# Row sums of a softmax: their guard taken from a constant array instead of an immediate number

## The chip, the cores and the metric

The kernel runs on one core of a Trainium2 chip. The metric is device time in microseconds (us) from one execution of the whole program, given as the median of several runs; lower is better. The engines are TensorE (PE, with its weight loads as PEld), VectorE (DVE), ScalarE (ACT), GpSimd (POOL) and SyncE (SP), which here only issues DMA transfers.

## The reference

Attention with a window of 32 positions to either side and 32 global tokens, for 8 batches of 8 heads with 512 local tokens and a head size of 64, followed by a feed-forward network on all 4352 rows. Every softmax divides by its row sum plus a guard of 1e-9:

```python
def sm(s):
    s = s - np.max(s, axis=-1, keepdims=True)
    e = np.exp(s)
    return e / (np.sum(e, axis=-1, keepdims=True) + 1e-09)

out_g = sm(scale * q_g @ k_all.T) @ v_all
out_l = sm(concat([scale * q_l @ k_g.T, where(mask, scale * q_l @ k_l.T, -1e9)])) @ v_all
x = concat([out_g, out_l])            # heads joined: rows of 512
h = x @ w_in                          # 512 -> 2048
out = (h - np.tanh(h)) @ w_out        # 2048 -> 512
```

## The kernel before

All arithmetic is in float32. TensorE multiplies each float32 operand as a rounded part and a remainder (`x_hi`, `x_lo`, `w_in_hi`, `w_in_lo`, `w_out_hi`, `w_out_lo`, and `gates` in both parts), three products to one. The weights are split once, in the first sixth of the program.

Attention goes by head pairs. The first four pairs (eight heads) go one way: `add_local_scores` multiplies queries with keys for tiles of 128 rows and 224 columns; `add_scores` has DVE take the row maxima with the mask (`peak`, line 1104), ACT take the exponent with the row sums as a by-product (`exp`, line 1111), and then `add_norms` lets DVE add the guard to the row sums and invert them (`inverse`, lines 671 and 672), for a pair of heads and two tiles at once: 128 partitions by 2 by 2 numbers. POOL multiplies the rows with the inverses (`norm`, line 1117), and TensorE transposes them (line 1176). The other 28 pairs go another way: `add_band_scores` and `add_band` do the same for one head and its four row tiles of 128 columns (`peak` line 1132, `exp` line 1137, `inverse` lines 1141 and 1142 on 128 by 4 numbers, `norm` line 1146, and a transpose on DVE, line 1152). The rows of the global tokens have their own path (`Quad`, lines 982 to 1050), whose guard is added together with a second sum, by an instruction with two arrays and an immediate (lines 997 and 1046).

The feed-forward network of a batch runs beside the attention of the next one: line 1219 (or 1245 at the start) multiplies by the first weights, ACT takes the tanh (line 1227), DVE subtracts (line 1230), ACT and POOL split the result in two parts (lines 363 and 1236), line 1282 multiplies by the second weights. When the last head is done, only the network is left, from about 780 us on.

The order of the work on every engine is worked out while the program is built: every operation is put in by `add` with the engines that can do it and its estimated time, due time, the keys that it reads (`r`) and writes (`w`), and the planner (`Order.run`) places them one after the other. An operation with `lock=True`, and each one on POOL, is planned so as not to run beside another such one. `inverse` is one with `lock=True`. Where TensorE would have to wait long in the first 72 us, the planner puts in multiplications of an identity (line 1509) as filling.

All tiles stand in one pool, one after the other in each partition, in the order of the code: `stats` (the maxima, sums and inverses) is the first, `idr`, `rawkq` and the others follow. In the built program `stats` starts at byte 640 of the partition, `idr` at 896, `rawkq` at 1408.

Of the kernel before, what the change touches and what calls it, by code (L numbers as in the profile page):

```python
# [8 lines left out]
F32 = mybir.dt.float32  # L9
# [4 lines left out]
ALU = mybir.AluOpType  # L14
PSUM = bass.MemoryType.PSUM

P = 128
D = 64
# [5 lines left out]
def f32(ap):  # L24
    return ap.bitcast(F32)


def view(ap, dims, off=0):

    return bass.AP(ap.tensor, ap.offset + off, [list(ap.ap[0])] + [list(d) for d in dims])  # L30
# [19 lines left out]
class Order:  # L50
# [19 lines left out]
    def add(self, eng, fn, due, r=(), w=(), res=(), alloc=(), free=(), lat=0.0, xfer=0.0, rows=1.0, ldw=0.107, tail=0.226, lock=False, mode=0):  # L70
        o = Op()
        engs = [x + (0.0,) * (3 - len(x)) + (lock,) * (len(x) < 4) for x in (eng if isinstance(eng, list) else [eng])]
        o.eng = {x[0]: x[1:3] for x in engs}

        o.lock = {x[0] for x in engs if x[3] or x[0] == "P"}
        o.xfer, o.rows, o.ldw, o.tail, o.mode, o.land = xfer, rows, ldw, tail, mode, self.land
        o.fn, o.due, o.lat, o.alloc, o.free = fn, due, lat, alloc, free
        o.n, o.ready, o.succ, o.start, o.args, o.seq = 0, dict.fromkeys(o.eng, 0.0), {}, None, {}, len(self.ops)
        before = {}
        for k in tuple(r) + tuple(w) + tuple(res):  # L80
            if k in self.writer:
                before[id(self.writer[k])] = self.writer[k]
        for k in tuple(w) + tuple(res):
            for x in self.readers.get(k, ()):
                before[id(x)] = x
        for x in before.values():
            x.succ[id(o)] = o
            o.n += 1
        for k in r:
            self.readers.setdefault(k, []).append(o)  # L90
        for k in w:
            self.writer[k] = o
            self.readers[k] = []
        self.ops.append(o)
        return o
# [122 lines left out]
def kernel(ctx, tc, q_l, k_l, v_l, q_g, k_g, v_g, w_in, w_out, out):  # L218
    nc = tc.nc
    B, H, S, _ = q_l.shape  # L220
    G = q_g.shape[2]
    NT = S // P
# [6 lines left out]
    cp = ctx.enter_context(tc.tile_pool(name="cp", bufs=1))  # L229
# [7 lines left out]
    SQ = 4 * G  # L237
    stats_all = cp.tile([P, 4, 16], F32, name="stats")
    stats = [stats_all[:, j] for j in range(4)]
    idr = cp.tile([P, P], F32R, name="idr")  # L240
    idn = f32(idr)

# [114 lines left out]
    add = order.add  # L357
# [107 lines left out]
    def outside(x):  # L465
        return view(x[:, 0, 0:1], [(NT * KC - 2 * 32, 2), (1, 32)])
# [33 lines left out]
    class Pair:  # L500
# [163 lines left out]
        def add_norms(self, p):  # L664
            both = stats_all[:, self.heads[0].sn:self.heads[0].sn + 2]
            for a in self.heads:
                a.add_scores(p)

            def inverse(e, _):
                x, y = [both[:, :, a + 2 * p:a + 2 * p + 2] for a in (4, 8)]  # L670
                nc.vector.tensor_scalar(x, x, 1e-9, None, op0=ALU.add)
                nc.vector.reciprocal(y, x)

            n = [a.norms for a in self.heads]
            add(("D", 0.37), inverse, n[0][1] - 0.5, r=[x[3] for x in n], w=[x[2] for x in n], lock=True)
            for norm, due, st, x in n:
                add(("P", 0.89), norm, due, r=[st], w=[x])

# [385 lines left out]
    class Head:  # L1064
# [61 lines left out]
        def add_band(self, pair):  # L1126
            s, p, st = (f"s{self.two}", self.i), f"p{self.two}0", ("st0", self.sn)
            x = probs[self.two].rearrange("p (t c) -> p t c", t=NT)

            def peak(e, _):  # L1130
                for t in range(NT):
                    nc.vector.tensor_tensor_reduce(out=x[:, t], in0=self.scores[:, t], in1=bands[0 if t == 0 else 2 if t == NT - 1 else 1],  # L1132
                                                   scale=-0.125, scalar=1e30, op0=ALU.add, op1=ALU.min, accum_out=self.st[:, t:t + 1])

            def exp(e, _):
                for t in range(NT):
                    nc.scalar.activation(x[:, t], x[:, t], AF.Exp, bias=self.st[:, t:t + 1], scale=-1.0, accum_out=self.st[:, 4 + t:5 + t])  # L1137

            def inverse(e, _):
                y = self.st[:, 4:8]  # L1140
                nc.vector.tensor_scalar(y, y, 1e-9, None, op0=ALU.add)
                nc.vector.reciprocal(self.st[:, 8:12], y)  # L1142

            def norm(e, _):
                for t in range(NT):
                    nc.gpsimd.tensor_scalar(x[:, t], x[:, t], self.st[:, 8 + t:9 + t], 1.0, op0=ALU.mult, op1=ALU.mult)  # L1146

            def turn(e, _):
                y = pair.squares()
                n = 4 // len(y)  # L1150
                for k, z in enumerate(y):
                    nc.vector.transpose(z[:, :, self.two].rearrange("p n t c -> p t n c"),  # L1152
                                        x[:, :, k * n * G:(k + 1) * n * G].rearrange("p t (n c) -> p t n c", c=G))

            def d(off):
                return self.due(self.C["o_l"] + self.C["o_lp"] + off)

            add(("D", 0.95), peak, d(1), r=[s] + [("band", j) for j in range(3)], w=[p, st], free=[(s, 1)])
            add(("A", 1.64), exp, d(1.5), r=[st], w=[p])
            add(("D", 0.38), inverse, d(2), r=[p], w=[st], lock=True)  # L1160
            add(("P", 1.45), norm, d(2.5), r=[st], w=[p])
            add(("D", 0.77 if pair.early else 0.71), turn, d(3), r=[p], w=pair.sqk, res=["rq1"] if pair.early else ())

# [165 lines left out]
    def add_constants():  # L1329
        def identity(e, _):  # L1330
            make_identity(nc, pg[:, :P])

        def rounded(e, _):
            nc.vector.tensor_copy(idr, pg[:, :P])
            nc.vector.memset(view(pg[:, :1], [(544, 2), (1, G)]), 0.0)

        def mask(j):
            def fn(e, _):
                m = masks[j]
                nc.gpsimd.memset(m, 0.0)  # L1340
                if j != 1:
                    c0, c1 = (0, 32) if j == 0 else (WIN - 32, WIN)
                    nc.gpsimd.memset(m[:, c0:c1], BIG)
                nc.gpsimd.affine_select(out=m[:, :WIN], in_=m[:, :WIN], pattern=[[1, WIN]], base=0,
                                        channel_multiplier=-1, compare_op=ALU.is_ge, fill=BIG)
                nc.gpsimd.affine_select(out=m[:, :WIN], in_=m[:, :WIN], pattern=[[-1, WIN]], base=64,
                                        channel_multiplier=1, compare_op=ALU.is_ge, fill=BIG)
            return fn

        def zeros(e, _):  # L1350
            for t in prob + prob2:
                nc.vector.memset(t[:, KC:], 0.0)

        def before_values(e, _):
            nc.vector.memset(first_rows[:32, 0, 0], 0.0)


        def edges(e, _):
            for x in first_kw:
                nc.vector.memset(outside(x), 0.0)  # L1360

        def global_ends(e, _):
            nc.vector.memset(first_gq, 0.0)

        def still(e, _):
            nc.vector.memset(f32(gates[:, 0, 0, 0]), 0.0)

        def warm(e, tags):
            x = gates[:, 0, 0, 0]
            for j in range(8):  # L1370
                nc.tensor.matmul(bank([P, 4, P], tags["warm"]), x, x.unsqueeze(1).broadcast_to([P, 4, P]), start=True, stop=True)

        add(("D", 0.15), still, -2000, w=["gh0"])
        add(("T", 1.71), warm, -2000, r=["gh0"], w=["warm"], alloc=[("warm", None)], free=[("warm", 1)])
        add(("P", 0.75), identity, -109, w=["pg0", "pg1", "pl0", "pl1"])
        add(("D", 0.3), rounded, -109, w=["idr", "pg0", "pg1", "pl0", "pl1"])
        add(("D", 0.3), edges, -108, w=["pw0", "pw1", "kw0"])
        add(("D", 0.1), before_values, -107, w=["vh0", "vh1"])
        add(("D", 0.3), global_ends, -106, w=["fm"])
        add(("D", 0.4), zeros, -97, w=["p00", "p10", "p01", "p11"])  # L1380
        for j in range(3):
            add(("P", (1.3, 1.1, 1.65)[j]), mask(j), -96, w=[("mask", j)])
# [6 lines left out]
    def attention(j):  # L1389
# [19 lines left out]
        if j % 2:  # L1409
            x.add_values()  # L1410
            x.add_global_turn()
            x.add_products(0, 1)

    add_constants()
    add_first_globals(0)
    pairs = [Pair(j) for j in range(NH // 2)]
# [129 lines left out]
```

## Time and profile before

| | us |
|---|---|
| median of 3 runs | 904.38 (903.88 to 907.87) |
| the profiled execution, its own time | 905.91 |
| its span, first to last instruction | 904.1 |
| mean granted clock of TensorE, share of full | 0.993 |

The span of the profiled execution is 1.8 us shorter than its time; the rest lies ahead of the first and behind the last instruction. The share of busy time by engine is 99% for PE, 53% for DVE, 41% for ACT and 37% for POOL. A busy PE is one with matmuls in flight; twelve matmuls of 128x512 take about 2.72 us, one after the other, throughout the program. Rows of the trace name an instruction by its line in the kernel, its output and its inputs.

### The profile page before, as it was taken

How to read it: one execution, taken by the hardware profiler on the slowest of the kernel's cores; microseconds unless marked ns; L12 is line 12 of the kernel's file. 1: busy time of each engine (PE TensorE's matmuls, PEld its weight loads, DVE VectorE, ACT ScalarE, POOL GpSimd, SP SyncE). 2: the span in 40 equal slices, each digit the busy share in tenths (PEclk: the TensorE clock that was granted, in tenths of full speed). 3: DMA queues.
4: the chain of work that ended last, by engine and by line, in shares of the span. 5: the costliest groups of instructions: out<-in, count | busy, mean ns of one | idle time of the engine just before them, and what ended most of it. 6: DMA issues, size and time to landing. Idle time of an engine off the chain costs nothing.

```text
span 904.1 us, 23449 instructions
## 1 busy us (share of the span) xinstructions
PE 892.7 (99%) x9100; PEld 719.8 (80%) x9100; DVE 481.7 (53%) x1820; ACT 372.5 (41%) x1035; POOL 338.9 (37%) x504
## 2 busy tenths in 40 slices
PE   8999999999999999999999999999999999999998
PEld 6678787787878888787878888788878888888896
DVE  6889977835638383745638373746637362111110
ACT  6877764434344333533343333533344242322221
POOL 5567665333333233333333233423223231222121
PEclk9899999999999999999999999999999999999999
DMA  9877774934555434555555434545454302100000
GB/s 207 192 185 204 205 182 98 226 92 112 107 135 139 101 85 112 142 117 116 103 153 116 109 84 111 144 114 119 95 147 112 95 35 61 47 1 1 36 13 23
DMA packets 286959, 101.14 MB, mean 112 GB/s; under 512 B 254848, under 2 KB 277376, under 8 KB 286848
## 3 DMA queue, kind: packets, MB, share of 16 engines
q1 hardware_dynamic: 284800, 98.53, 45.5%
q8 instruction: 71, 1.16, 0.5%
q10 hardware_dynamic: 2048, 1.11, 0.4%
q14 instruction: 40, 0.33, 0.1%
HBM read 76.01 MB, written 21.50 MB: 108 GB/s over the span
## 4 chain that ended last, share of the span: by engine, by line
PE 92%; DVE 4%; ACT 2%; issue 1%; DMA 1%; POOL 0%; ACTq 0%; DVEq 0%; POOLq 0%
PE bank L1282 40%; PE bank L1219 39%; PE bank L830 4%; PE bank L730 3%; PE bank L814 2%; PE bank L1245 1%; PE bank L656 1%; PE bank L1176 1%; PE bank L972 1%; DVE turned L793 1%; DVE stats L977 1%; DMA raw<-in_q_l_dram 1%; DVE t L1230 0%; ACT prob L1137 0%; PE bank L547 0%
## 5 line engine op out<-in xcount | busy, mean ns | idle before, releaser
L1236 POOL TENSOR_TENSOR gates<-t,gates 128x512 fp32r<-128x512 f32 x136 | 175.1, 1288 | 394.0 <-PE bank L1282 245.7
L1282 PE MATMUL bank<-w_out_hi,gates 128*128 128x512 f32 x1088 | 297.2, 393 | 0.9 <-ACT gates L363 0.9
L1282 PEld LDWEIGHTS bank<-w_out_hi,gates 128*128 128x128 f32 x1088 | 202.3, 188 | 46.9 <-issue 2.9
L1230 DVE TENSOR_TENSOR t<-bank,t 128x512 f32<-128x512 f32 x136 | 92.8, 684 | 238.8 <-ACT t L1227 238.3
L1227 ACT ACTIVATE t<-bank 128x512 f32<-128x512 f32 x136 | 80.7, 594 | 232.2 <-PE bank L1219 231.2
L363 ACT CAST gates<-t 128x512 fp32r<-128x512 f32 x136 | 84.3, 622 | 166.9 <-PE bank L1282 92.8
L1282 PE MATMUL bank<-w_out_lo,gates 128*128 128x512 f32 x544 | 150.8, 391 | 0.0
L1219 PE MATMUL bank<-x_hi,w_in_hi 128*128 128x512 f32 x432 | 123.4, 401 | 0.0
L1282 PEld LDWEIGHTS bank<-w_out_lo,gates 128*128 128x128 f32 x544 | 102.0, 188 | 21.8 <-issue 0.2
L1219 PE MATMUL bank<-x_lo,w_in_hi 128*128 128x512 f32 x432 | 118.6, 390 | 0.0
L1219 PE MATMUL bank<-x_hi,w_in_lo 128*128 128x512 f32 x432 | 118.5, 390 | 0.0
L1146 POOL TENSOR_SCALAR prob<-prob,stats 128x128 f32<-128x128 f32 x224 | 79.0, 372 | 82.5 <-DVE stats L1142 43.7
L1137 ACT ACTIVATE prob<-prob,stats 128x128 f32<-128x128 f32 x224 | 86.9, 390 | 22.8 <-DVE stats L1132 22.8
L1219 PEld LDWEIGHTS bank<-x_lo,w_in_hi 128*128 128x128 f32 x432 | 81.0, 188 | 17.7 <-issue 0.2
L1219 PEld LDWEIGHTS bank<-x_hi,w_in_lo 128*128 128x128 f32 x432 | 80.9, 188 | 17.8 <-issue 0.2
L1219 PEld LDWEIGHTS bank<-x_hi,w_in_hi 128*128 128x128 f32 x432 | 77.8, 188 | 19.3 <-issue 2.8
L793 DVE STREAM_TRANSPOSE turned<-pg 32x96 f32<-32x96 f32 x288 | 77.7, 270 | 8.5 <-PE bank L830 1.7
L1132 DVE CUSTOM_DVE_ANT_0 prob<-bank,band 128x128 f32<-128x128 f32 x224 | 49.7, 286 | 28.1 <-PE bank L730 28.1
L1152 DVE STREAM_TRANSPOSE sq<-prob 128x512 f32<-128x512 f32 x50 | 35.3, 708 | 51.3 <-POOL prob L1146 48.7
L1137 ACT ACTIVATION_READ_ACCUMULATOR prob<-prob,stats 128x1 f32 x224 | 42.1, 188 | 0.0
L830 PEld LDWEIGHTS bank<-turned 128*32 128x32 f32 x3072 | 33.4, 111 | 8.9 <-issue 5.7
L830 PE MATMUL bank<-turned 128*32 128x32 f32 (+1 forms) x3072 | 37.2, 206 | 0.1
(157 smaller groups left out, 900.1 us busy)
## 6 DMA issues: line engine op xcount, KB each, us to landing
moved<-sq SPq DMA_DIRECT2D x24, 512.0 KB, 2.8
turned<-in_v_l_dram SPq DMA_DIRECT2D x23, 512.0 KB, 5.4
turned<-in_v_l_dram SPq DMA_DIRECT2D x32, 256.0 KB, 3.5
out_dram<-wraw SPq DMA_DIRECT2D x32, 256.0 KB, 2.1
rawkq<-in_k_l_dram SPq DMA_DIRECT2D x112, 64.0 KB, 2.6
rawkq<-in_q_l_dram SPq DMA_DIRECT2D x112, 64.0 KB, 2.4
turned<-in_v_g_dram SPq DMA_DIRECT2D x48, 128.0 KB, 4.6
turned<-moved SPq DMA_DIRECT2D x48, 128.0 KB, 2.9
```

The lines of the kernel that those rows point to most:

```text
L363: (nc.scalar.copy if e == "A" else eng[e].tensor_copy)(dst, src)
L793: nc.vector.transpose(win_g[G * g:G * g + G, a.two, 3 * x:3 * x + 3], view(pgh[r, a.two, G * (j + x):G * (j + x) + 1], [(3 * G, 3), (1, G)]))
L830: m = nc.tensor.matmul(y, win_v[:, NW * a.two + w, G * d:G * d + G], x, start=n == 0, stop=n == 7, skip_group_check=True)
L1132: nc.vector.tensor_tensor_reduce(out=x[:, t], in0=self.scores[:, t], in1=bands[0 if t == 0 else 2 if t == NT - 1 else 1], scale=-0.125, sc ...
L1137: nc.scalar.activation(x[:, t], x[:, t], AF.Exp, bias=self.st[:, t:t + 1], scale=-1.0, accum_out=self.st[:, 4 + t:5 + t])
L1146: nc.gpsimd.tensor_scalar(x[:, t], x[:, t], self.st[:, 8 + t:9 + t], 1.0, op0=ALU.mult, op1=ALU.mult)
L1152: nc.vector.transpose(z[:, :, self.two].rearrange("p n t c -> p t n c"), x[:, :, k * n * G:(k + 1) * n * G].rearrange("p t (n c) -> p t n ...
L1219: nc.tensor.matmul(self.h[s][:, j * n:(j + 1) * n], w[:, cc, f * P:(f + 1) * P], self.x()[xi](cc)[:, :n], start=part == 0 and cc == 0 and ...
L1227: nc.scalar.activation(tt_[q], self.h[s], AF.Tanh)
L1230: nc.vector.tensor_sub(tt_[q], self.h.pop(s), tt_[q])
L1236: eng[e].tensor_sub(gg[q][1], tt_[q].rearrange("p (k c) -> p k c", k=4), f32(gg[q][0]))
L1282: nc.tensor.matmul(self.acc[tt], g[:, j * nt + tt], low_out(f) if wi else w_out_hi[:, f], start=s == 0 and k == 1, stop=last and k == 3 * ...
```

## The change

In the two functions named `inverse` whose guard was an instruction of its own, `tensor_scalar` with the immediate 1e-9 becomes `tensor_tensor` with a second array: `guard`, a new tile of 128 partitions by one number, read over and over with step zero. The first place is built 8 times, the second 56 times. `guard` is set once, by a `memset` on DVE, in the operation that also clears the operand of the first multiplications (`still`), behind that one's memset. The two operations now also read the key `guard`.

```diff
     stats_all = cp.tile([P, 4, 16], F32, name="stats")
     stats = [stats_all[:, j] for j in range(4)]
+    guard = cp.tile([P, 1], F32, name="guard")
     idr = cp.tile([P, P], F32R, name="idr")
...
             def inverse(e, _):
                 x, y = [both[:, :, a + 2 * p:a + 2 * p + 2] for a in (4, 8)]
-                nc.vector.tensor_scalar(x, x, 1e-9, None, op0=ALU.add)
+                nc.vector.tensor_tensor(x, x, guard.unsqueeze(1).broadcast_to([P, 2, 2]), op=ALU.add)
                 nc.vector.reciprocal(y, x)
...
-            add(("D", 0.37), inverse, n[0][1] - 0.5, r=[x[3] for x in n], w=[x[2] for x in n], lock=True)
+            add(("D", 0.37), inverse, n[0][1] - 0.5, r=[x[3] for x in n] + ["guard"], w=[x[2] for x in n], lock=True)
...
             def inverse(e, _):
                 y = self.st[:, 4:8]
-                nc.vector.tensor_scalar(y, y, 1e-9, None, op0=ALU.add)
+                nc.vector.tensor_tensor(y, y, guard.broadcast_to([P, NT]), op=ALU.add)
                 nc.vector.reciprocal(self.st[:, 8:12], y)
...
-            add(("D", 0.38), inverse, d(2), r=[p], w=[st], lock=True)
+            add(("D", 0.38), inverse, d(2), r=[p, "guard"], w=[st], lock=True)
...
         def still(e, _):
             nc.vector.memset(f32(gates[:, 0, 0, 0]), 0.0)
+            nc.vector.memset(guard, 1e-9)
...
-        add(("D", 0.15), still, -2000, w=["gh0"])
+        add(("D", 0.15), still, -2000, w=["gh0", "guard"])
```

In the built program the sequence of instructions on PE, ACT, POOL and SP is the same, and so is what each of them waits for. On DVE one memset is added, as the second instruction, and 64 instructions change their kind in place, with the same waits. The new tile takes 32 bytes of each partition, so `idr` and every tile behind it start 32 bytes later: `rawkq` at 1440 instead of 1408, and so on to the end. All of them but two masks started at a multiple of 128 bytes before.

## Rows read from the trace of the kernel before

**Rows 1.** Busy us (share of the span) x instructions, by engine, from the page:

```profile
PE 892.7 (99%) x9100; PEld 719.8 (80%) x9100; DVE 481.7 (53%) x1820; ACT 372.5 (41%) x1035; POOL 338.9 (37%) x504
```

**Rows 2.** Stretches of the span: length, busy time by engine, clock, DMA share, GB/s.

```profile
0.00:62.00 62.00, 55.80 (x450) 41.88 (x451) 48.11 (x204) 46.73 (x133) 35.16 (x71) 0.92 0.87 201
62.00:115.00 53.00, 52.99 (x373) 41.89 (x372) 47.48 (x142) 38.78 (x104) 39.27 (x48) 1.00 0.73 198
200.00:780.00 580.00, 579.85 (x6853) 466.73 (x6852) 309.87 (x1218) 216.63 (x634) 196.45 (x303) 1.00 0.46 109
```

**Rows 3.** Chain that ended last, 0 to 66 us: start, length, what.

```profile
1.86 4.95 DMA raw<-in_q_l_dram
...
15.62 0.09 DVE stats L671
...
17.80 0.81 DVE stats L671
...
18.63 0.19 DVE stats L672
...
18.91 0.89 POOL prob L1117 x2
...
35.88 0.09 DVE stats L671
...
38.11 0.09 DVE stats L671
```

**Rows 4.** Lines by instruction, DVE: duration ns min/median/max, first and last start.

```profile
L671 DVE TENSOR_SCALAR stats<-stats x8: 158/162/796, 15.5 to 48.8; 128x4 f32<-128x4 f32 x8
...
L1141 DVE TENSOR_SCALAR stats<-stats x56: 104/149/1001, 65.1 to 729.0; 128x4 f32<-128x4 f32 x56
...
L1142 DVE RECIPROCAL stats<-stats x56: 177/178/181, 65.3 to 729.1; 128x4 f32<-128x4 f32 x56
...
L988 DVE TENSOR_TENSOR stats<-stats x12: 160/161/163, 157.1 to 733.4; 128x2 f32<-128x2 f32 x12
...
L1046 DVE SCALAR_TENSOR_TENSOR stats<-stats x4: 119/156/1046, 16.9 to 115.1; 128x1 f32<-128x1 f32 x4
```

**Rows 5.** Groups by line, DVE: busy us, mean ns of one.

```profile
L1492 DVE TENSOR_TENSOR turned<-xg,turned 128x256 fp32r<-128x256 f32 x4 | 1.7, 426 | 0.1
...
L1352 DVE MEMSET t<- 128x32 f32 x4 | 0.2, 85 | 0.0
```

**Rows 6.** Timeline of DVE, then POOL, three places: start us, us.

```profile
17.80 0.80 DVE L671 TENSOR_SCALAR stats<-stats 128x4 f32<-128x4 f32 x1 [0.57 <-ACT t L1111]
...
17.80 0.77 POOL L1050 TENSOR_SCALAR pg<-pg,stats 128x608 f32<-128x608 f32 x1
...
37.24 0.88 POOL L1117 TENSOR_SCALAR t<-t,stats 128x224 f32<-128x224 f32 x2
...
72.36 1.05 DVE L1046 SCALAR_TENSOR_TENSOR stats<-stats 128x1 f32<-128x1 f32 x1
...
72.10 2.54 POOL L1236 TENSOR_TENSOR gates<-t,gates 128x512 fp32r<-128x512 f32 x2
...
701.32 1.00 DVE L1141 TENSOR_SCALAR stats<-stats 128x4 f32<-128x4 f32 x1
...
701.01 1.28 POOL L1236 TENSOR_TENSOR gates<-t,gates 128x512 fp32r<-128x512 f32 x1 [0.35 <-ACT gates L363]
```

**Rows 7.** Waits, by pair: us in total, times, longest; PE alone from 66 us on.

```profile
PE bank L1282 <- ACT gates L363: 0.6, 1, 0.6
PE bank L814 <- issue: 0.2, 1, 0.2
```

**Rows 8.** DMA issues by line: count, KB each, median us from issue to landing.

```profile
rawkq<-in_k_l_dram SPq DMA_DIRECT2D x112, 64.0 KB, 2.6
...
turned<-moved SPq DMA_DIRECT2D x96, 64.0 KB, 2.2
```

## The prediction

> **What bounds the kernel now.** The busy times come first: PE works for 99% of the span and DVE for 53% [rows 1], so an instruction on DVE counts only where PE waits for it. The stretches tell where that can be: from 62 us on PE is busy without a gap (52.99 of 53.00, later 579.85 of 580.00), while in the first 62 us it lacks 6.2 of 62.00 [rows 2]. The waits say the same from the other side: from 66 us to the end all that PE itself waited for is 0.8 us, 0.6 of it for ACT and 0.2 for issuing, nothing for DVE [rows 7]. So the 56 guards of line 1141, all from 65 us on, lie beside full work of PE, and the 8 of line 671, all before 49 us [rows 4], lie in the one stretch that is not full. The chain that ended last decides which of those eight count: in its first 66 us line 671 stands four times, at 15.62, 17.80, 35.88 and 38.11 us, three times with 0.09 us and once with 0.81 [rows 3]. The reader is to see in the timeline what that 0.81 is: at 17.80 us POOL starts a multiplication of 0.77 us, and the guard on DVE, which is issued at that moment, takes 0.80 instead of its median of 0.162 us [rows 4, 6].
>
> **The 64 instructions.** What is removed takes 162 ns at line 671 and 149 ns at line 1141, by the medians [rows 4]. What is added, a tensor_tensor of 4 columns with both inputs in SBUF, is not in the trace. The nearest row has 2 columns and takes 161 ns (line 988, with both inputs in SBUF, 160 to 163 over twelve) [rows 4]; the same kind with 256 columns takes 426 ns (line 1492) [rows 5], so a column costs (426 - 161) / 254 = 1.04 ns, and 4 columns come to 161 + 2 x 1.04 = 163 ns. The first place then changes by 8 x (163 - 162) = 0.01 us, the second by 56 x (163 - 149) = 0.8 us of DVE time, spread over 660 us. On the path lie the four of the first place: 4 x 1 ns, nothing. The bounds: the shortest guard of before took 104 ns [rows 4], so the new one can be longer by 163 - 104 = 59 ns at most, 4 x 0.059 = 0.24 us on the path; as a gain I allow the same.
>
> [...]
>
> **The wait for POOL.** The guard of before is stretched where POOL is in the middle of something: 796 ns at the worst at line 671, and 1001 at line 1141, there with a POOL instruction from 701.01 to 702.29 us and the guard from 701.32 to 702.32 [rows 4, 6]. The reciprocal right behind it is not: 177 to 181 ns over 56 [rows 4]. The question is whether the new kind waits too. No tensor_tensor with both inputs in SBUF met a POOL instruction, but the nearest kind with two arrays in SBUF did: line 1046 took 1046 ns at 72.36 us instead of 156, behind POOL's line 1236 [rows 4, 6]. So I take it that the new guard waits as the old one did, at the same places, and the term is 0. Its bounds: if it never waits, the guard at 17.80 us ends 0.80 - 0.16 = 0.64 us earlier, but what follows it is POOL's line 1117, and POOL is held by its own multiplication until 17.80 + 0.77 = 18.57 us. It started at 18.91 [rows 3, 6], so the chain gains 0.34 us. If the new kind waits where the old one did not, there is one such place on the path: at 38.03 us POOL still has 0.09 us to go (line 1117, from 37.24 for 0.88) [rows 6], and 0.09 us is the loss.
>
> **What covers the other 56.** They are followed by the reciprocal, POOL's multiplication and a transpose, and TensorE needs these for a head long after; its cover is the network's matmuls, which fill 579.85 of 580.00 us [rows 2]. If that cover were gone at every place, the price would be the whole 0.8 us. Nothing else is queued differently: the waits of each instruction are the same, and the reciprocal stands behind the guard as before.
>
> **The memset.** It is one more instruction on DVE in the first two microseconds; the nearest is 85 ns for 32 columns [rows 5]. It stands behind the memset that the first multiplications wait for, and they wait for that one alone. Behind it are memsets whose results are needed microseconds later, when the first loads have landed: the chain's first link is a load until 6.81 us [rows 3]. I take 0; without that cover it would be 0.09 us.
>
> **The move by 32 bytes.** Every tile behind the statistics starts 32 bytes later. No row shows an engine or a DMA slower at one multiple of 32 bytes than at another, because nearly all tiles stood at multiples of 128. I take 0 and price the other case among the rivals.
>
> **The sum.** Central 0.00 us. The known terms reach from -0.24 - 0.34 = -0.58 to 0.24 + 0.09 + 0.09 + 0.8 = 1.22 us. Against the profiled execution that is 905.91 us (904.1 of span and 1.8 around it) unchanged; that execution lay 1.5 us over the median of the runs, so for the median I forecast the 904.4 us of before. A measurement of this kernel tells about 0.5%, 4.5 us, from no change.
>
> **Rivals.** (a) *The new kind doesn't wait for POOL.* The stretched guards would then belong to the one-array kind alone. The four places on the path then give 0.34 us back at most, and later ones nothing since PE is full: 904.0 us. Against it stands line 1046, with two arrays and a wait of 1046 ns [rows 4, 6]. [...]
>
> (b) *The transfers get slower, and the kernel with them.* Its place is the first 62 us, where the DMA engines are busy for 0.87 of the time [rows 2] with short pieces: the loads of `rawkq` come in rows of 32 numbers, 128 bytes. If a piece that starts 32 bytes off takes longer in SBUF, the stretch becomes one of the DMA engines from a factor of 1 / 0.87 = 1.15 on; 4.5 us are lost at (62.0 + 4.5) / (62.0 x 0.87) = 1.23. The nearest rows for a price of finer pieces: 64 KB in pieces of 128 bytes land in 2.6 us, 64 KB in pieces of 1024 bytes (`moved` to `turned`) in 2.2 [rows 8], 1.18 for eight times as many pieces. At 1.18 the stretch would be 62.0 x 0.87 x 1.18 = 63.6 us and the time 906.0, still no difference; both landings hold a fixed part, though, so the factor can be larger. At 1.3 the stretch is 70.1 us and the time 904.4 + 8.1 = 912.5. For it speaks only that nothing in the trace excludes it; against it, that the factor must be over 1.23, and that the later stretches have room (shares of 0.73 and 0.46).
>
> (c) *The chain of the first 62 us falls otherwise.* Guards a few ns earlier or later meet POOL in another order, and one wait of about 1 us, as at line 1046, is won or lost at one or two of the four places: 902.4 to 906.4 us, no difference that can be measured.
>
> **How the numbers follow.** No change by the sum above: 0.70; (a) 0.09; (c) 0.07, both within 0.5%; (b) 0.09, all of it slower. A gain over 0.5%, from the same move with its sign turned (loads that land sooner), gets 0.05. That makes 0.05 faster, 0.86 same, 0.09 slower. The time is 904.4. The range: the sum's own ends are 903.8 and 905.6, (c) gives 902.4 and 906.4, and runs of one kernel reach from 903.88 to 907.87, so the median of a few can lie some 1.5 us higher than the one known. I give 902.6 to 907.2, and leave (b) and the gain outside.
>
> **What would show it.** Line 1141's successor with a median between 149 and 165 ns and some at up to 1.0 us beside POOL (none over 0.25 us beside a running POOL instruction would be rival a); the four places of the chain as before, with 0.8 us at about 17.80; twelve matmuls in 2.72 us; a first stretch that has PE at the end of its first network multiplications at the same time; DMA shares of 0.87 and 0.73, and 2.6 us for `rawkq` (larger: rival b). I am wrong if PE loses time after 66 us, or if the DMA shares of the first 115 us rise.

## The result and the profile after

| | before | after |
|---|---|---|
| median of 5 runs, us | 905.50 (903.88 to 907.87) | 911.45 (910.29 to 914.16) |
| ratio | | 1.0068 [1.0054, 1.0082] |
| the profiled execution, its own time | 905.91 | 912.28 |
| its span | 904.1 | 910.5 |

The changed kernel is slower by 0.7%, 6 us, and outside the predicted range. Of the 12 runs of experiment 4 two, of 1760.93 and 3078.02 us, are left out of its median and its ratio. The stretches, against [rows 2] (length, busy us by engine, clock, DMA share, GB/s):

```profile
0.00:62.00 62.00, 52.82 (x447) 38.19 (x448) 47.23 (x205) 46.00 (x130) 34.70 (x71) 1.00 0.90 193
62.00:115.00 53.00, 51.89 (x367) 40.91 (x367) 45.74 (x137) 37.15 (x100) 38.00 (x47) 1.00 0.76 197
...
200.00:780.00 580.00, 576.12 (x6833) 463.09 (x6833) 309.40 (x1216) 214.24 (x632) 195.13 (x301) 1.00 0.57 109
```

From 200 to 780 us PE was busy for 579.85 of 580.00 us and now lacks 3.88. The DMA engines move the same 109 GB/s there, but are busy for 0.57 of the time instead of 0.46. Over the whole span the queue that carries nearly all transfers has the same 284800 packets and 98.53 MB, and a share of 53.7% instead of 45.5%. The first stretch can't be compared with [rows 2]: the clock granted to TensorE there was 0.92 in the profile of before and is 1.00 in this one. For such places experiment 1 below, which has the 64 new instructions and a clock of 1.00, is the better partner.

The two guards, by line (ns min/median/max, first and last start), against [rows 4]:

```profile
L672 DVE TENSOR_TENSOR stats<-stats,guard x8: 151/157/784, 13.6 to 48.7; 128x4 f32<-128x4 f32 x8
...
L1142 DVE TENSOR_TENSOR stats<-stats,guard x56: 99/142/997, 65.6 to 735.4; 128x4 f32<-128x4 f32 x56
```

They are 5 and 7 ns shorter by the median than the ones they replace, and stretched up to 784 and 997 ns as these were (796 and 1001), again beside POOL. The longest, DVE and then POOL (start us, us; in brackets idle before it):

```profile
707.72 1.00 DVE L1142 TENSOR_TENSOR stats<-stats,guard 128x4 f32<-128x4 f32 x1
...
707.41 1.30 POOL L1237 TENSOR_TENSOR gates<-t,gates 128x512 fp32r<-128x512 f32 x1 [0.35 <-ACT gates L364]
```

The transfers did change. Issues by line (count, KB each, median us to landing), against [rows 8]:

```profile
turned<-in_v_l_dram SPq DMA_DIRECT2D x23, 512.0 KB, 6.6
...
out_dram<-wraw SPq DMA_DIRECT2D x32, 256.0 KB, 3.0
rawkq<-in_k_l_dram SPq DMA_DIRECT2D x112, 64.0 KB, 2.9
rawkq<-in_q_l_dram SPq DMA_DIRECT2D x112, 64.0 KB, 3.3
turned<-in_v_g_dram SPq DMA_DIRECT2D x48, 128.0 KB, 6.4
```

The same five in the kernel before:

```profile
turned<-in_v_l_dram SPq DMA_DIRECT2D x23, 512.0 KB, 5.4
...
out_dram<-wraw SPq DMA_DIRECT2D x32, 256.0 KB, 2.1
rawkq<-in_k_l_dram SPq DMA_DIRECT2D x112, 64.0 KB, 2.6
rawkq<-in_q_l_dram SPq DMA_DIRECT2D x112, 64.0 KB, 2.4
turned<-in_v_g_dram SPq DMA_DIRECT2D x48, 128.0 KB, 4.6
```

`turned` takes the values in rows of 64 numbers, 256 bytes, and `rawkq` in rows of 128 bytes. In the trace's packet records a packet of 256 bytes (121280 of them) takes 19.5 ns on average before and 27.9 after, one of 128 bytes (121856) 12.6 and 13.8, one of 4096 bytes 191 and 192. All packets together take 6749 us before and 7994 after, spread over 16 engines: a factor of 1.18. The output's transfers (`out_dram`) go in packets of 2048 bytes, 89.9 ns before and 94.3 after, 5% more, and still land 0.9 us later, 43% more.

What PE waited for from 200 to 780 us (us in total, times, longest):

```profile
PE bank L831 <- DVE turned L796: 3.8, 5, 1.6
```

This is nearly all of the 3.88 us. Line 831 multiplies the values with the transposed rows of a head pair, 128 matmuls at a time and four times in a batch; the five waits fall on the one of the four that follows the copies of a batch's outputs. In the kernel before no wait of PE is listed in this stretch. The question is how slower transfers come to make DVE late. ACT's waits in the same stretch hold one that grew, here after the change:

```profile
ACT wraw L364 <- DMA out_dram<-wraw: 7.0, 5, 2.6
```

and here before it:

```profile
ACT wraw L363 <- DMA out_dram<-wraw: 2.5, 2, 1.7
```

ACT copies a finished output into `wraw`, from which SP sends it off; the next copy has to wait until the transfer before it has read the tile.

### The profile page after: what moved, and what is told of

It reads as the page before. It is cut to its first block, busy times and chain, and to the rows that moved or that the text cites. A ratio compares the mean times of both kernels' runs of the same rounds, so it can differ in the third digit from the quotient of the medians.

```text
span 910.5 us, 23450 instructions
## 1 busy us (share of the span) xinstructions
PE 891.1 (98%) x9100; PEld 716.6 (79%) x9100; DVE 481.8 (53%) x1821; ACT 371.8 (41%) x1035; POOL 339.7 (37%) x504
## 3 DMA queue, kind: packets, MB, share of 16 engines
q1 hardware_dynamic: 284800, 98.53, 53.7%
q10 hardware_dynamic: 2048, 1.11, 0.5%
## 4 chain that ended last, share of the span: by engine, by line
PE 81%; DVE 8%; DMA 5%; ACT 3%; issue 2%; POOL 1%; SPq 1%; ACTq 0%; DVEq 0%; POOLq 0%
PE bank L1283 36%; PE bank L1220 35%; PE bank L831 4%; PE bank L731 3%; DMA out_dram<-wraw 2%; DVE stats L978 1%; DVE turned L794 1%; PE bank L815 1%; DMA wraw<-in_moe_w_in_dram 1%; DVE t L1231 1%; POOL gates L1237 1%; DMA wraw<-in_moe_w_out_dram 1%; PE bank L973 1%; ACT t L1228 1%; DMA first_q<-in_moe_w_out_dram 1%
```

## The experiments

The theory formed from this: the move of the tiles by 32 bytes makes rows of 256 bytes slower to write, and later transfers wait. Its rivals: the 64 instructions cost the time by themselves, or another tile than `turned` does. Ratios are to the kernel before, timed on the same chip, with a 95% interval; medians of 5 to 12 runs.

**1. The instructions without the move.** The guard's tile is widened to 256 bytes and 256 bytes are taken from a reserve that lies ahead of the tiles, so that every tile behind `guard` stands where it stood before:

```diff
-    guard = cp.tile([P, 1], F32, name="guard")
+    guard = cp.tile([P, 64], F32, name="guard")[:, :1]
...
-    nc = _bacc.Bacc(..., dynamic_dma_scratch_size=512)
+    nc = _bacc.Bacc(..., dynamic_dma_scratch_size=256)
```

> The changed kernel with a guard tile of 256 bytes and the reserved area at the bottom of SBUF (for descriptors that this program does not use) cut from 512 to 256 bytes: idr and all tiles behind it stand at the very addresses of before, and the 64 tensor_tensor instructions and the memset are what is left of the change. If the whole loss is the move: ratio within 0.999 to 1.001, 904.5 to 906 us, DMA share 45.5%. If the instructions carry the rest (after against the move alone was 0.13%, the guard behind 0.19%): ratio 1.001 to 1.002, 906 to 907 us.

904.85 us, 0.9997 [0.9988, 1.0005]; DMA share of the queue 45.6%, PE busy 579.76 of 580 us. The 64 new instructions and the memset cost nothing that can be measured. Its first stretch is the partner of the changed kernel's:

```profile
0.00:62.00 62.00, 52.85 (x448) 37.90 (x449) 47.24 (x205) 45.84 (x130) 34.69 (x71) 1.00 0.86 197
```

The DMA share is 0.86 there, against 0.90 with the move, and PE is busy for the same time (52.85 and 52.82).

**2. The move without the instructions.** The kernel before, with a tile that nobody uses:

```diff
     stats = [stats_all[:, j] for j in range(4)]
+    pad = cp.tile([P, 1], F32, name="pad")
```

> The kernel before with one unused tile of 4 bytes at the place where the changed kernel has its guard: every tile behind the statistics starts 32 bytes later, the 64 instructions are those of before. Theory 'the move': the whole loss of 0.68% is here, 910 to 913 us, and the DMA queue's share of 16 engines rises from 45.5% to about 53.7% for the same packets. Rival 'the new instructions' (other waits between DVE and POOL): 904 to 907 us and a share near 45.5%.

909.95 us, 1.0055 [1.0040, 1.0070]; share 53.8%, PE 575.88. The move alone does it; its interval overlaps that of the whole change.

**3. The guard behind the large tiles.** The changed kernel, with the line of `guard` put behind the tiles of `bands`, so that only three small ones (`kw`, `hi0`, `x_lo1b`) move:

```diff
-    guard = cp.tile([P, 1], F32, name="guard")
     idr = cp.tile([P, P], F32R, name="idr")
...
+    guard = cp.tile([P, 1], F32, name="guard")
```

> The changed kernel with the guard's tile behind all tiles but kw, hi0 and x_lo1b, so that every tile that a transfer from HBM writes stands where it stood before; the 64 tensor_tensor instructions stay. Theory 'the move': 904 to 907 us, DMA share near 45.5%, guards of 142 to 157 ns by the median and up to 1.0 us beside POOL. Rival 'the new instructions': 910 to 913 us.

906.36 us, 1.0019 [1.0008, 1.0029]; share 45.4%, PE 579.89. The loss is gone but for 0.2%. **4.** To see whether that rest is the instructions or the three tiles, the kernel before with 32 bytes ahead of these three:

```diff
+    pad = cp.tile([P, 8], F32, name="pad")
```

> The kernel before with 32 bytes of padding behind the bands, so that kw, hi0 and x_lo1b alone start 32 bytes later. The guard's tile at this place, with the 64 new instructions, took 1.0019 of before, and the instructions alone 0.9997. If these three tiles carry it: 1.001 to 1.003, 906 to 907.5 us. If that was chance or an interplay: 0.999 to 1.001, 904.5 to 906 us.

906.28 us, 1.0013 [1.0001, 1.0024]; share 45.5%. The interval ends at the edge of no difference. By the ratio the three tiles cost about a fifth of the loss, and not by way of the transfers. From 200 to 780 us PE is full here too, but gets through 6849 matmuls, as in experiment 3, instead of 6853 [rows 2]:

```profile
200.00:780.00 580.00, 579.93 (x6849) 466.05 (x6848) 309.68 (x1218) 216.35 (x634) 195.86 (x302) 1.00 0.47 109
```

Compared matmul by matmul with experiment 1, both runs fall behind by about 1 us from 200 us on, 0.97 us of it, in both, at the 363 matmuls of `x_hi` with `w_in_lo`: from one start to the next 232.7 ns instead of 230.0 (worked out from the starts of the matmuls in the traces). Where tiles stand thus changes PE's own pace a little; why, and which of the three does it, was not found.

**5 and 6. A move by 64 and by 128 bytes.** The changed kernel with a wider guard:

```diff
-    guard = cp.tile([P, 1], F32, name="guard")
+    guard = cp.tile([P, 16], F32, name="guard")[:, :1]
```

> The changed kernel with a guard tile of 64 bytes a partition: all tiles behind it start 64 instead of 32 bytes later than before. If a transfer is slowed only by starting off a multiple of 64 bytes: 904 to 907 us, share near 45.5%. If a row of 256 bytes must start at a multiple of 128 or 256 to be quick: 910 us or more and a share over 50%. Rival 'the new instructions': 910 to 913 us with a share near 45.5%.

909.89 us, 1.0051 [1.0034, 1.0067]; share 53.0%, PE 576.12.

```diff
+    guard = cp.tile([P, 32], F32, name="guard")[:, :1]
```

> The changed kernel with a guard tile of 128 bytes: all tiles behind it start 128 bytes later than before, those that started at a multiple of 256 (turned, pg, first_q) now at 128 past one, and rawkq, wraw01 and raw3 the other way round. If multiples of 64 or 128 are enough: 904 to 907 us, share near 45.5%. If a row of 256 bytes must lie on a multiple of 256: turned, which takes the most rows, is slowed and the time is 908 us or more.

905.25 us, 1.0006 [0.9994, 1.0018]; share 48.9%, PE 578.94. The move by 64 bytes doesn't help, the one by 128 does, though its share lies between the others and the 256-byte packets take 23.3 ns.

**7. The tile `turned` and what lies behind it, moved by 32 bytes.** The kernel before with

```diff
+    pad = cp.tile([P, 8], F32, name="pad")   # ahead of turned
```

> The kernel before with 32 bytes of padding ahead of the tile turned alone: turned (rows of the values, 256 bytes each, most of all packets of that size) and the small tiles behind it start 32 bytes later; rawkq, wraw01, raw3, first_q stay. Theory 'rows of 256 bytes to turned carry the loss': DMA share 51 to 53.5%, 907 to 910 us, the loss from 200 us on (some 4 us of idle PE) as in the move alone. Rival 'the loads of the first 100 us carry it': share under 48%, 904.5 to 906.5 us.

910.38 us, 1.0058 [1.0045, 1.0070]; share 53.0%, PE 576.45. **8. All but these.** 32 bytes behind `stats`, 224 ahead of `turned`, and the reserve shortened by 256, so that only what lies between is moved:

```diff
+    pad = cp.tile([P, 8], F32, name="pad")     # behind stats
+    pad2 = cp.tile([P, 56], F32, name="pad2")  # ahead of turned
```

> The other half: the kernel before with the reserved area cut to 256 bytes, 32 bytes of padding ahead of idr and 224 ahead of turned: everything between statistics and turned starts 32 bytes past the multiple it had, turned and what is behind it at the addresses of before. Theory 'turned carries the loss': share 45.5 to 48%, 904.5 to 907 us, PE full from 200 us on. Rival 'the first loads': 908 to 910 us, lost before 100 us.

907.15 us, 1.0019 [1.0008, 1.0030]; share 45.9%, PE 579.88. Most of the loss comes with `turned`, in rows of 256 bytes, and what lies behind it; the tiles ahead of it, among them `rawkq`, which rival (b) of the prediction named, have a small part (packets of 128 bytes 13.0 ns here, those of 256 bytes 19.7). The two parts add up to 0.0077, above the 0.0055 of both at once, within their intervals. Either half also has slower matmuls of `x_hi` with `w_in_lo` after 200 us, 0.95 us in all in experiment 7 and 0.64 in experiment 8 against experiment 1, which the move of everything together has not. So it is not shown that the transfers to `rawkq` cost anything.

**9. `turned` and what lies behind it, moved by 128 bytes.**

```diff
+    pad = cp.tile([P, 32], F32, name="pad")   # ahead of turned
```

> The kernel before with 128 bytes of padding ahead of turned alone: its rows of 256 bytes start 128 past a multiple of 256, all ahead of it stays. By the whole move of 128 (share 48.9%, no loss, but other tiles gained): share 48 to 49.5% and 906.5 to 908.5 us if the loads ahead gained 2 to 3 us there, as the run with all at 256 suggests; 905 to 906 us if turned at 128 costs nothing.

905.27 us, 1.0004 [0.9994, 1.0014]. The queue's share of 48.5% is as expected for a `turned` that suffers, but the 906.5 to 908.5 us that were to go with it are a miss. Packets of 256 bytes take 23.0 ns, two fifths of the surcharge, and the share from 200 to 780 us is 0.51; PE still has 578.99 us there. Line 831 waits for 1.0 us in all instead of 3.8, and ACT's wait ahead of it lies between those of before (2.5) and after (7.0):

```profile
ACT wraw L364 <- DMA out_dram<-wraw: 4.1, 5, 1.7
```

So the price isn't in proportion to the transfers' time: at a share of 0.51 most of it is hidden, at 0.57 it isn't. That the time shows no loss at all is partly luck: compared matmul by matmul with experiment 1 this run loses 0.03 us in all after 200 us, since other matmuls follow one another faster, as in experiments 11 and 12.

**10. The transfers by themselves.** A kernel that loads values into tiles at offsets of 0, 32, 64, 96 and 128 bytes, in rows of 256 bytes (`wide`) and of 128 (`narrow`), with nothing beside them:

> Nothing of the reference is computed (the output is zeros). Eight stretches one after the other, each of four transfers of 512 KB from HBM into a tile that starts at a multiple of 256 bytes, at an offset in it: rows of 256 bytes at offsets 0, 32, 64, 96 and 128 (tiles wide_a to wide_e), then rows of 128 bytes at 0, 32 and 64 (narrow_f to narrow_h). If what counts is where a row starts in SBUF: offsets 0 the fastest, 32, 64 and 96 alike and some 1.4 times as long by packet (from 19.5 to 27.9 ns, before to after), 128 between or like 0; rows of 128 bytes 1.1 times as long at 32 and 64 as at 0. If the move only counts together with the load of the real kernel: all offsets within 5%.

Issues by line, offsets 0, 32, 64, 96, 128 for `wide` and 0, 32, 64 for `narrow` (count, KB each, median us to landing):

```profile
wide_a<-in_v_l_dram SPq DMA_DIRECT2D x4, 512.0 KB, 5.5
wide_b<-in_v_l_dram SPq DMA_DIRECT2D x4, 512.0 KB, 6.7
wide_c<-in_v_l_dram SPq DMA_DIRECT2D x4, 512.0 KB, 6.7
wide_d<-in_v_l_dram SPq DMA_DIRECT2D x4, 512.0 KB, 6.8
wide_e<-in_v_l_dram SPq DMA_DIRECT2D x4, 512.0 KB, 6.7
narrow_f<-in_v_l_dram SPq DMA_DIRECT2D x4, 512.0 KB, 6.5
narrow_g<-in_v_l_dram SPq DMA_DIRECT2D x4, 512.0 KB, 8.9
narrow_h<-in_v_l_dram SPq DMA_DIRECT2D x4, 512.0 KB, 9.0
```

The reader is to see 5.5 against four times 6.7 to 6.8, close to the 5.4 and 6.6 that the kernels show. The mean packet of 256 bytes takes 18.0, 24.1, 24.0, 23.8 and 23.5 ns, that of 128 bytes 13.0, 21.5 and 21.5. So of the five offsets the rows of 256 bytes are cheap only at the one where they start at multiples of 256 (18.0 ns), and how far off they start makes hardly a difference when the transfers are alone (23.5 to 24.1). The rows of 128 bytes that start at multiples of 128 are cheap: every second row of `narrow_f` starts 128 past a multiple of 256, and 15998 of its 16384 packets take 13 ns. In the two cheap cases of the eight the rows start at multiples of their own length and cross no multiple of 256; which of the two counts was not separated. Two parts of the expectation missed: the offset of 128 is as dear as the others here, and the narrow rows are dearer than thought, 1.65 times, where the kernel's own packets of 128 bytes went from 12.6 to 13.8 ns only. What makes these differ inside the kernel was not found.

**11 and 12. Everything at multiples of 256.** The kernel before with the reserve shortened by 256 and 128 bytes added at two places, so that `rawkq`, `wraw` and the others that stood at odd multiples of 128 come to stand at multiples of 256, and `turned` stays:

```diff
+    pad = cp.tile([P, 32], F32, name="pad")    # behind stats
+    pad2 = cp.tile([P, 32], F32, name="pad2")  # ahead of first_q
```

> The kernel before with the reserved area cut to 256 bytes, 128 bytes of padding ahead of idr and 128 ahead of first_q: the tiles that started 128 past a multiple of 256 (rawkq, wraw01, sq, raw3, raw4, first_kq and others) start at a multiple of 256, first_q and turned where they were. If multiples of 256 count for rows of 256 bytes and more: share 43 to 45%, 902 to 904.5 us, below the kernel before. If 128 is enough for these: 904.5 to 906 us and 45.5%.

902.16 us, 0.9967 [0.9954, 0.9980]: faster than the kernel before. The queue's share is 45.2%, just above the 43 to 45% expected. The first stretch has a DMA share of 0.81:

```profile
0.00:62.00 62.00, 53.73 (x447) 39.98 (x448) 47.75 (x204) 47.06 (x133) 35.32 (x72) 0.95 0.81 199
...
200.00:780.00 580.00, 579.76 (x6860) 468.17 (x6859) 309.70 (x1218) 216.83 (x635) 196.37 (x303) 1.00 0.46 109
```

But in this profile the gain isn't made in the first stretch. Matmul by matmul, this run is 0.5 us behind the kernel before at 62 us, level at 100 us, 0.4 ahead at 281, 1.0 at 483 and 2.2 at the end, with PE full in both: it gets through 6860 matmuls from 200 to 780 us instead of 6853. Of the 2.1 us won after 200 us, 1.2 lie at line 1282, where matmuls with `w_out_lo` start 227.0 ns apart instead of 228.6. So this gain lies in PE's own pace; why the pace changes was not found.

The same in the changed kernel, with the guard's tile as the first of the two (`[P, 32]`, its first column used):

> The changed kernel with all large tiles at multiples of 256 as in the run that did so for the kernel before (guard in a tile of 128 bytes, reserved area 256 bytes, 128 bytes ahead of first_q). If the instructions are free: 901.5 to 903 us, as there (902.2). If they cost something that the addresses hid: 903.5 to 905 us.

903.16 us, 0.9979 [0.9969, 0.9988]; share 45.4%. With its tiles placed so, the change comes out faster than the kernel before. Its profile is 1.6 us ahead of experiment 1 at 200 us and 3.3 at the end, so half is again won in PE's pace; whether the transfers win the other half was not separated.

**13 and 14. The copy of the output set free.** This tests the path from the transfers to PE. In both kernels the output is sent from a tile that nobody rewrites (a part of the weights), at the same size; ACT still copies into `wraw`, but has nothing to wait for. The edit frees SP as well: in the changed kernel SP waited 30.8 us for this copy from 200 to 780 us, in 11 times, before it sent the output and what stands behind it in its order. The times can't tell these two apart; the timelines below show which one counts:

```diff
-                            y = wraw[key[1]]
+                            y = f32(w_out_hi[:, 0])
```

The kernel before with it:

> The kernel before, whose transfers to the output read a weight tile in SBUF that nothing writes at that time instead of wraw (the output holds weights, not results): the same transfers, but no copy into wraw waits for one. Both theories: 903 to 906 us, since the wait of ACT for these transfers was 6.2 us in all with PE full; this is the yardstick for the next run.

904.63 us, 0.9996 [0.9987, 1.0006]; share 45.4%, PE 579.78. The changed kernel with it:

> The changed kernel with the same edit (the output holds weights, not results). Theory 'ACT's copy waits for the output's transfer, and tanh, DVE and TensorE stand behind it': PE idle from 200 to 780 us falls from 3.9 to under 1 us, and the time lies 1 to 3 us above that of the yardstick instead of 6. Rival 'TensorE waits for the rows of turned themselves': 3 to 4 us of idle PE there and 5 to 7 us above the yardstick.

906.28 us, 1.0007 [0.9998, 1.0016]. The queue's share is 53.7%, as high as in the changed kernel itself, and the stretch reads

```profile
200.00:780.00 580.00, 579.83 (x6853) 467.07 (x6852) 309.19 (x1218) 216.46 (x635) 195.89 (x303) 1.00 0.58 112
```

The transfers are as slow as ever (0.58), and PE is full: 579.83. What is left of the loss is 906.28 - 904.63 = 1.65 us instead of 6 (by the ratios 1.0 us). Matmul by matmul, experiment 14 is 1.95 us behind experiment 13 at 200 us and 1.84 at the end, so nothing is lost after 200 us. The timelines show that the loss there goes through the wait of ACT. The changed kernel near 272 us, ACT (start us, us; in brackets idle before it):

```profile
272.31 0.59 ACT L364 COPY wraw<-bank 128x512 f32<-128x512 f32 x1 [1.76 <-DMA out_dram<-wraw]
272.80 0.60 ACT L1228 ACTIVATE t<-bank 128x512 f32<-128x512 f32 x1
```

DVE behind it:

```profile
273.44 0.69 DVE L1231 TENSOR_TENSOR t<-bank,t 128x512 f32<-128x512 f32 x1 [1.90 <-ACT t L1228]
...
282.47 1.77 DVE L794 STREAM_TRANSPOSE turned<-pg 32x96 f32<-32x96 f32 x6
284.27 0.20 DVE L796 STREAM_TRANSPOSE turned<-pg 32x32 f32<-32x32 f32 x1
```

and PE:

```profile
284.52 1.56 PE L831 MATMUL bank<-turned 128*32 128x64 f32 x128 [1.57 <-DVE turned L796]
```

Experiment 1 has the same instructions at the same place, ACT:

```profile
269.03 0.57 ACT L364 COPY wraw<-bank 128x512 f32<-128x512 f32 x1
269.87 0.60 ACT L1228 ACTIVATE t<-bank 128x512 f32<-128x512 f32 x1 [0.27 <-PE bank L1220]
```

There the copy goes at once, and the tanh (line 1228) waits for PE alone. In the changed kernel the copy stands 1.76 us waiting for the output's transfer, and the tanh behind it in ACT's order with it, although its input has been ready. DVE's subtraction waits for the tanh, and in DVE's order everything behind it, up to the transposes that feed line 831, comes as much later. PE idles for 1.57 us. The other four waits of line 831, at 386.18 (0.40 us), 488.87 (1.38), 590.31 (0.20) and 694.03 us (0.30), have the same some 12 us ahead of them:

```profile
373.97 0.59 ACT L364 COPY wraw<-bank 128x512 f32<-128x512 f32 x1 [0.60 <-DMA out_dram<-wraw]
...
476.67 0.59 ACT L364 COPY wraw<-bank 128x512 f32<-128x512 f32 x1 [1.57 <-PE bank L973]
...
578.11 0.59 ACT L364 COPY wraw<-bank 128x512 f32<-128x512 f32 x1 [0.42 <-DMA out_dram<-wraw]
...
681.49 1.08 ACT L364 COPY wraw<-bank 128x512 f32<-128x512 f32 x2 [2.58 <-DMA out_dram<-wraw]
```

The second is put down to PE by the profile, because PE's semaphore rose last, at 476.60 us; the transfer that the copy waited for had landed at 476.57. In experiment 1 only the last of the four copies has a wait of note, 1.25 us.

## Why the prediction was wrong

**The instructions: right.** 163 ns were forecast; 157 and 142 were measured, and experiment 1 puts all 64 with their memset at 0.9997. Beside POOL they take up to 784 and 997 ns, as the old ones did (796 and 1001). The chain's place at 17.80 us in [rows 3] is there again, 1.9 us earlier in this profile, where TensorE's clock in the first 62 us was 1.00 instead of 0.92:

```profile
15.89 0.80 DVE stats L672
```

That refutes rival (a). The memset at nothing was right as well, and experiment 1 shows no sign of rival (c). The prediction's own signs of being wrong both came: PE loses 3.88 us after 200 us, and the DMA shares of the first two stretches are 0.90 and 0.76, against 0.86 and 0.72 in experiment 1.

**The step that failed** is the term for the move by 32 bytes, "I take 0". The reason given was that no row shows a transfer slower at one multiple of 32 bytes than at another, because nearly all tiles stood at multiples of 128. That is a reason to know nothing, not one for zero. Experiment 2 measures the term at 0.55%, 5.0 us.

**Rival (b)** is what happened, at a chance of 0.09. Its cause holds: rows that start 32 bytes off take longer, 1.43 on a packet of 256 bytes (27.9 / 19.5), 1.18 over all packets. So does its fixed part in a landing: of the output, 256 KB land in 2.1 us by the median in the kernel before, 64 KB in 1.8. Two parts of its working don't.

- *Its place.* It looked to the first 62 us and to `rawkq`. There a factor of 1.18 was to cost 1.6 us. Matmul by matmul, the changed kernel lies behind experiment 1 (both with a clock of 1.00) by 0.1 us at 62 us, by 1.1 us at 77 us and by 1.4 us at 161 us (worked out from the starts of their matmuls), so the size is fair, but the first 62 us don't show it. This is rough: the profile of experiment 4 lies 2.1 us ahead of experiment 1 at 62 us, with no quicker transfers. Experiment 14 leaves 1.65 us, about the same. And most of the loss comes with `turned` and what lies behind it, by experiments 7 and 8.
- *That "the later stretches have room" (0.73 and 0.46).* About three quarters of the loss came from there, in steps: the delay is 1.4 us at 161 us, 2.9 at 281, 3.3 at 382, 4.6 at 483, 5.0 at 680 and 5.8 at 695, then it stays. The five waits of line 831, 3.8 us, make most of it. A mean share of 0.57 leaves room for bytes, but it doesn't tell how long one transfer stands behind others at one moment. The wait was to be read before already: ACT waited for `out_dram<-wraw` twice, 1.7 us at the longest, without PE noticing. The prediction named what stands behind the changed instructions on DVE, and did not ask which waits for transfers stood close to being late.

**The cover failed in the same way.** The prediction took it that a full PE covers what DVE loses. 579.85 of 580.00 us [rows 2] says that nothing was late; it does not say by how much. Experiment 9 shows the margin: with a DMA share higher by a tenth (0.51 / 0.46) PE loses 579.85 - 578.99 = 0.9 us there, with one higher by a quarter (0.57 / 0.46), as after the change, 3.7.

**What stays open:** why the place of tiles changes PE's pace in experiments 3, 4, 11 and 12; which waits make up the 1.4 us that are lost ahead of 161 us; and why a move by 128 bytes costs two fifths of the surcharge in the kernel and nearly all of it alone.

## What to carry to other kernels

A new tile, however small, moves every tile behind it: widen it so that these keep their places (experiment 1, with the reserve shortened to match: no loss), or at least so that tiles which transfers write in rows of 256 bytes keep starting at multiples of 256 (such a row took 19.5 ns here, and 27.9 when it started 32 bytes off). Nearly last in the order, the tile still cost 0.2% here (experiment 3). Other places are worth trying by themselves (902.16 us against 905.33 here), though in the two profiles at least half of that gain came through PE's own pace, which the transfers don't foretell. A full engine shows no margin (PE, busy for 579.85 of 580.00 us before, lost 3.7 after the change), nor does a mean DMA share (0.46 before, 0.57 after): look for the waits for transfers that stand in the order of an engine ahead of work the full engine needs, and ask how much later they may come.

## What was not expected of the hardware

- In experiment 10 a row of 256 bytes written to SBUF at an offset of 32, 64, 96 or 128 bytes from a multiple of 256 takes 23.5 to 24.1 ns instead of 18.0, one of 128 bytes at 32 or 64 takes 21.5 instead of 13.0, with nothing beside them. In the kernel, 32 bytes off, it is 27.9 instead of 19.5 ns and 13.8 instead of 12.6.
- After the move, transfers whose own packets cost nearly the same (2048 bytes, 94.3 ns instead of 89.9) landed later too: 256 KB from `wraw` to the output in 3.0 us instead of 2.1.
- Rows of 128 bytes were as cheap 128 past a multiple of 256 as on one: 13 ns for 15998 of 16384 packets (experiment 10).
- A full PE was faster or slower by where tiles stand: 6849 to 6860 matmuls in the same 580 us without a wait, in programs that differ from each other in the places of tiles alone (experiments 4 and 11).
- The instruction with two SBUF arrays of 4 columns wasn't dearer than the one with an immediate: 142 ns against 149, 157 against 162, by the median.
